# Two matrix products on one tensor engine: their matmuls put one by one in turn, with one order of passes for both

## The chip, the cores and the metric

The kernel runs on one core of a Trainium2 chip. A core has a tensor engine (PE; its loads of the stationary operand are shown apart as PEld), a vector engine (DVE, VectorE), a scalar engine (ACT, ScalarE), GpSimd (POOL), the sync engine's DMA queue (SP), and two on-chip memories: SBUF for operands and PSUM, eight banks into which the tensor engine accumulates. The metric is the device time of one execution in microseconds, as the median of several runs.

## The reference

For each of 4 batches with 6080 tokens of 256 channels, q and k are normalised over the tokens, a 256 x 256 attention over channels is formed and applied to v, and the 24320 resulting rows go through a feed-forward layer with 2048 hidden units and an ELU:

```python
qn = q / (np.linalg.norm(q, axis=1, keepdims=True) + 1e-06)
kn = k / (np.linalg.norm(k, axis=1, keepdims=True) + 1e-06)
a = softmax(kn.transpose(0, 2, 1) @ qn / tau)      # 256 x 256 a batch
x = (v @ a).reshape(24320, 256)
h = x @ w_in                                       # 256 -> 2048
g = np.where(h > 0.0, h, np.exp(np.minimum(h, 0.0)) - 1.0)
out = g @ w_out                                    # 2048 -> 256
```

## The kernel before

(v @ a) @ w_in is computed as v @ (a @ w_in), so each batch needs its own W' = a @ w_in (tiles `wp`). The tokens are cut into 12 chunks a batch, 8 of 512 tokens and 4 of 496, and a chunk is worked on in 16 *steps*, one for each 128 of the 2048 hidden units. There are 48 x 16 = 768 steps. The first three chunks take their first 8 steps one chunk after the other and then the last 8, while the weights are still being converted from 64-bit floats (`convert_w_in`, `convert_w_out`, on DVE and ACT).

The large products are made of three passes. Every operand is split into a high and a low part (`split`, L70 to L72: ACT casts the high part, DVE subtracts to get the low one), and high x high, high x low and low x high are added up in PSUM. A step i consists of:

- the first product, `h_item`: for each of two halves of the 256 channels three matmuls (L297 to L299) into a PSUM tile `ph`, whose stationary operand is a part of W' and whose moving operand is a part of v's chunk (`vt`);
- `elu`: on odd steps, and in all steps of the first three chunks, ACT computes a Relu and an Exp (L308, L309) and DVE joins them with ph (L310); on the others ACT computes one Exp (L312) and DVE does two operations (L313, L314). The last of these is the last reader of ph;
- `split_g` of the step before: ACT casts `e` to g's high part (L71), DVE subtracts to get g's low part (L72);
- the second product, `out_item`, of step j = i - 3 (LAG = 3): for each of two halves of the 256 outputs three matmuls (L334 to L336) into the PSUM tiles `po`, with w_out's parts (`wo`) as the stationary operand and g's as the moving one;
- after a chunk's last step, `store`: two copies out of po (L351; L347 and L349 in a few chunks) and the output DMAs.

Beside these, *side work* for the next batch is hung on some steps: row groups of q and k (24 a batch: a square and a split on ACT, a sum and a split on DVE: L120, L124, L71, L72; then `gram` matmuls, L142 and L145), the softmax over channels (L164 to L216), and the W' products (`pw`, L256 to L260). The loads of all these are issued by SP.

PSUM's eight banks are shared out as two for gram, three for the ring `w` (ph, pw and the softmax's small tiles) and three for the ring of po, two of which a chunk uses.

The program order is that of the loop at the end of the kernel. The framework then orders each engine's instructions by its own estimate of when they can start, so the order on ACT and DVE isn't exactly that of the code. Each engine runs its instructions strictly in order and waits at each for the semaphores of the engines that it depends on.

Of the kernel before, what the change touches and what calls it, by code (L numbers as in the profile page):

```python
# [7 lines left out]
F32 = mybir.dt.float32  # L8
# [6 lines left out]
# The high words of float64's 2**-126 and of the largest below 2**128, as float32 bits.  # L15
# [13 lines left out]
def channel_attention_then_elu_ffn(ctx: ExitStack, tc, q, k, vT, tau, w_in, w_out, outT):  # L29
    """out = elu((v @ softmax(kn^T qn / tau)) @ w_in) @ w_out.  # L30

    (v @ a) @ w_in is computed as v @ (a @ w_in): a is only C x C per batch.
    float32 operands of the large products are split exactly into two float32r
    parts, x = hi + lo (12 significant bits each), and three passes carry
    hi*hi + hi*lo + lo*hi. w_in and w_out come as the bits of float64 numbers
    and are rounded to float32 here. vT and outT have channels first: C x (B * N).
    """
# [14 lines left out]
    # The first M chunks take the first half of F, one after the other, and then the second:  # L52
    # w_out and half of w_in are converted while they run.
# [21 lines left out]
    def to_f32(dst, pair, act=False):  # L75
        """dst [P, n] float32 from pair [P, n, 2] words, low word first."""
# [4 lines left out]
        # the magnitude, held within float32's normal range (the words compare as floats do)  # L81
# [6 lines left out]
        # sign and top exponent bit stay; three exponent bits go  # L88
# [60 lines left out]
    def keep_warm(n):  # L149
        """Products that nothing reads: the tensor engine's clock falls while it waits."""  # L150
# [117 lines left out]
    def span(c):  # L268
        """The chunk's batch, first token and length."""
# [20 lines left out]
    def h_item(c, f, vt):  # L290
        b, _, n = span(c)
        wp = wps[b]
        ph = ps.tile([P, CH], F32, tag="w", bufs=WB, name="ph")
        fs = slice(f * P, f * P + P)
        for kt in range(KT):
            hi, lo = (vt[:, kt, x, 0:n] for x in range(2))
            nc.tensor.matmul(ph[:, 0:n], wp[kt][:, 0, fs], hi, start=(kt == 0), stop=False)  # L297
            nc.tensor.matmul(ph[:, 0:n], wp[kt][:, 0, fs], lo, start=False, stop=False)  # L298
            nc.tensor.matmul(ph[:, 0:n], wp[kt][:, 1, fs], hi, start=False, stop=(kt == KT - 1))  # L299
        return ph  # L300

    def elu(c, ph, both):
# [3 lines left out]
        # h > 0: h >= exp(0) - 1; h <= 0: exp(h) - 1 >= h  # L306
# [22 lines left out]
    def out_item(c, f, g, po):  # L329
        n = span(c)[2]  # L330
        hi, lo = (g[:, x, 0:n] for x in range(2))
        for dt in range(DT):
            o, ds = po[dt][:, 0:n], slice(dt * P, dt * P + P)
            nc.tensor.matmul(o, wo[:, f, 0, ds], hi, start=first(c, f), stop=False)  # L334
            nc.tensor.matmul(o, wo[:, f, 1, ds], hi, start=False, stop=False)  # L335
            nc.tensor.matmul(o, wo[:, f, 0, ds], lo, start=False, stop=last(c, f))  # L336
# [53 lines left out]
    # the second W' buffer's room until batch 1 needs it  # L390
# [150 lines left out]
    for i in range(len(steps) + LAG):  # L541
        if i < len(steps):
            c, f = steps[i]
            ph = h_item(c, f, vts[c])
# [3 lines left out]
        j = i - LAG  # L548
        if j >= 0:
            c, f = steps[j]  # L550
            if first(c, f):
                pos[c] = [
                    ps.tile([P, CH], F32, tag="o", bufs=8 - KT - WB, name=f"po_{c}_{dt}") for dt in range(DT)
                ]
            out_item(c, f, gs.pop(j), pos[c])
            if last(c, f):
                store(c, f, pos.pop(c))
# [37 lines left out]
```

## Time and profile before

| | before |
|---|---|
| median of 3 runs | 2319.38 us (2317.86 to 2319.63) |
| span of the profiled execution | 2318.7 us |
| PE busy | 2307.7 us, 10296 matmuls |
| PEld busy | 1909.2 us, 10296 loads |
| DVE busy | 1539.6 us |
| ACT busy | 1479.0 us |
| DMA | 118.14 MB |

The profiled execution's own time is its span, 2318.7 us, from the first to the last instruction; the median of the runs is 0.7 us above it. In the timeline a row gives the start and the duration in us, the engine, the source line, the operation, out<-in, and, in square brackets, how long the engine had been idle before and what ended that. The matmuls' durations overlap, since they are pipelined: how fast they follow one another is read from their starts. In a group's row the number behind the bar's comma is the mean duration in ns, and the last column the idle time of the engine just before.

### The profile page before, as it was taken

Reading aid. Unit: us, or ns where it says so; the run is one execution under the profiler, and the core shown is the slowest. Engines: PE = TensorE matmul, PEld = TensorE weight load, DVE = VectorE, ACT = ScalarE, POOL = GpSimd, SP = SyncE. Lnnn points to the kernel's source line nnn. Section 1 sums busy time; section 2 is a strip of 40 time slices with the busy share of each in tenths; the row PEclk is TensorE's granted clock in tenths of the full one; section 3 lists DMA queues with packets and bytes.
Section 4 is the critical chain, followed back from the end, with each engine's and each line's share of the span. In section 5 each row is a group of like instructions: output and inputs, shape, how many; then the busy total and the mean of one; then the engine's idle time right before and its main releaser. Section 6 shows DMA issues by size and latency. Waiting matters only on the chain.

```text
span 2318.7 us, 27257 instructions
## 1 busy us (share of the span) xinstructions
PE 2307.7 (100%) x10296; PEld 1909.2 (82%) x10296; DVE 1539.6 (66%) x2400; ACT 1479.0 (64%) x2413; POOL 3.1 (0%) x10
## 2 busy tenths in 40 slices
PE   8999999999999999999999999999999999999999
PEld 7778888888888888888888888888888888888887
DVE  7976666666766666666666666666666566665565
ACT  5776666666656666666666666666666666666665
POOL 0000000000000000000000000000000000000000
PEclk9999999999999999999999999999999999999999
DMA  9311121111201111111111111121101000000000
GB/s 335 107 37 46 55 64 55 64 52 37 64 19 55 55 46 55 55 47 51 37 55 37 46 46 55 46 63 46 48 31 56 26 19 27 28 19 10 19 9 18
DMA packets 60947, 118.14 MB, mean 51 GB/s; under 512 B 6032, under 2 KB 15760, under 8 KB 60816
## 3 DMA queue, kind: packets, MB, share of 16 engines
q1 hardware_dynamic: 60816, 116.42, 15.4%
q8 instruction: 80, 1.31, 0.2%
q14 instruction: 51, 0.42, 0.1%
HBM read 89.39 MB, written 27.00 MB: 50 GB/s over the span
## 4 chain that ended last, share of the span: by engine, by line
PE 97%; DVE 1%; DMA 1%; issue 0%; SPq 0%; ACT 0%; DVEq 0%
PE po L335 15%; PE po L334 15%; PE ph L297 15%; PE po L336 15%; PE ph L299 15%; PE ph L298 15%; PE gram L142 3%; PE gram L145 1%; DVE acc L124 1%; PE pw L256 1%; PE pw L258 0%; PE pw L260 0%; PE pw L259 0%; DMA wi<-in_moe_w_in_dram 0%; DMA raw<-in_k_dram 0%; PE pn L164 0%
## 5 line engine op out<-in xcount | busy, mean ns | idle before, releaser
L71 ACT CAST g<-e 128x512 fp32r<-128x512 f32 (+1 forms) x768 | 472.1, 615 | 509.9 <-DVE e L314 282.7
L72 DVE TENSOR_TENSOR g<-e,g 128x512 fp32r<-128x512 f32 (+1 forms) x768 | 526.2, 685 | 345.7 <-ACT g L71 308.3
L335 PE MATMUL po<-g,wo 128*128 128x512 f32 (+1 forms) x1536 | 603.1, 393 | 0.0
L334 PE MATMUL po<-g,wo 128*128 128x512 f32 (+1 forms) x1536 | 599.9, 391 | 0.0
L336 PE MATMUL po<-g,wo 128*128 128x512 f32 (+1 forms) x1536 | 597.9, 389 | 0.0
L297 PE MATMUL ph<-vt,wp 128*128 128x512 f32 (+1 forms) x1504 | 589.1, 392 | 0.0
L299 PE MATMUL ph<-vt,wp 128*128 128x512 f32 (+1 forms) x1504 | 584.4, 389 | 0.0
L298 PE MATMUL ph<-vt,wp 128*128 128x512 f32 (+1 forms) x1504 | 583.8, 388 | 0.0
L310 DVE SCALAR_TENSOR_TENSOR e<-e,ph 128x512 f32<-128x512 f32 (+1 forms) x408 | 278.0, 681 | 315.6 <-ACT e L309 315.1
L308 ACT ACTIVATE e<-ph 128x512 f32<-128x512 f32 (+1 forms) x408 | 242.6, 595 | 170.9 <-PE ph L299 168.1
L336 PEld LDWEIGHTS po<-g,wo 128*128 128x128 f32 x1536 | 289.3, 188 | 61.6
L334 PEld LDWEIGHTS po<-g,wo 128*128 128x128 f32 x1536 | 288.4, 188 | 61.2 <-ACT wo L71 0.4
L335 PEld LDWEIGHTS po<-g,wo 128*128 128x128 f32 x1536 | 288.7, 188 | 58.6 <-DVE wo L72 0.2
L297 PEld LDWEIGHTS ph<-vt,wp 128*128 128x128 f32 x1504 | 282.3, 188 | 61.5 <-issue 0.5
L299 PEld LDWEIGHTS ph<-vt,wp 128*128 128x128 f32 x1504 | 282.6, 188 | 59.0
L298 PEld LDWEIGHTS ph<-vt,wp 128*128 128x128 f32 x1504 | 283.0, 188 | 53.9 <-issue 1.0
L312 ACT ACTIVATE e<-ph 128x512 f32<-128x512 f32 (+1 forms) x360 | 213.3, 592 | 90.9 <-PE ph L299 72.8
L309 ACT ACTIVATE e<-e 128x512 f32<-128x512 f32 (+1 forms) x408 | 256.5, 629 | 12.1
L314 DVE TENSOR_TENSOR e<-ph,e 128x512 f32<-128x512 f32 (+1 forms) x360 | 246.6, 685 | 10.9
L313 DVE TENSOR_SCALAR e<-e 128x512 f32<-128x512 f32 (+1 forms) x360 | 152.1, 423 | 57.7 <-ACT e L312 55.2
L142 PE MATMUL gram<-qk 128*128 128x512 f32 x288 | 106.4, 393 | 0.0
L124 DVE TENSOR_TENSOR acc<-acc,sq 128x1024 f32<-128x1024 f32 x80 | 97.7, 1221 | 11.6 <-ACT sq L120 11.5
(94 smaller groups left out, 1130.2 us busy)
## 6 DMA issues: line engine op xcount, KB each, us to landing
raw<-in_q_dram SPq DMA_DIRECT2D x92, 256.0 KB, 2.7
raw<-in_k_dram SPq DMA_DIRECT2D x92, 256.0 KB, 3.0
v<-in_v_dram SPq DMA_DIRECT2D x32, 512.0 KB, 3.7
out_dram<-o SPq DMA_DIRECT2D x58, 256.0 KB, 2.0
v<-in_v_dram SPq DMA_DIRECT2D x16, 496.0 KB, 3.6
out_dram<-o SPq DMA_DIRECT2D x32, 248.0 KB, 2.1
wraw<-w_scr SPq DMA_DIRECT2D x12, 512.0 KB, 3.3
wi<-in_moe_w_in_dram SPq DMA_DIRECT2D x4, 1024.0 KB, 8.7
```

Of the source, the lines that this page charges most:

```text
L71: nc.scalar.copy(hi, src)
L72: nc.vector.tensor_sub(lo, src, hi.bitcast(F32))
L297: nc.tensor.matmul(ph[:, 0:n], wp[kt][:, 0, fs], hi, start=(kt == 0), stop=False)
L298: nc.tensor.matmul(ph[:, 0:n], wp[kt][:, 0, fs], lo, start=False, stop=False)
L299: nc.tensor.matmul(ph[:, 0:n], wp[kt][:, 1, fs], hi, start=False, stop=(kt == KT - 1))
L308: nc.scalar.activation(ev, pv, AF.Relu, scale=-1.0)
L309: x = nc.scalar.activation(ev, ev, AF.Exp, scale=-1.0)
L310: y = nc.vector.scalar_tensor_tensor(ev, ev, -1.0, pv, op0=ALU.add, op1=ALU.max)
L314: y = nc.vector.tensor_tensor(ev, pv, ev, op=ALU.max)
L334: nc.tensor.matmul(o, wo[:, f, 0, ds], hi, start=first(c, f), stop=False)
L335: nc.tensor.matmul(o, wo[:, f, 1, ds], hi, start=False, stop=False)
L336: nc.tensor.matmul(o, wo[:, f, 0, ds], lo, start=False, stop=last(c, f))
```

## The change

`h_item` and `out_item` no longer issue their matmuls. They return them as lists of six calls, and a new function `weave` issues the two lists in turn: the first product's first matmul, the second product's first, the first's second, and so on. Where only one list is there (the first three steps, and the last three rounds of the loop), it is issued alone. The second product's three passes used to be high x high, low weight x high, high weight x low; they now stand in the first product's order, high x high, high weight x low, low weight x high. In the loop the matmuls of both products now stand ahead of `elu` and `split_g`, and `store` behind them. The numbers of matmuls, operands, tiles and buffers stay the same.

```diff
     def h_item(c, f, vt):
...
+        calls = []
         for kt in range(KT):
             hi, lo = (vt[:, kt, x, 0:n] for x in range(2))
-            nc.tensor.matmul(ph[:, 0:n], wp[kt][:, 0, fs], hi, start=(kt == 0), stop=False)
-            nc.tensor.matmul(ph[:, 0:n], wp[kt][:, 0, fs], lo, start=False, stop=False)
-            nc.tensor.matmul(ph[:, 0:n], wp[kt][:, 1, fs], hi, start=False, stop=(kt == KT - 1))
-        return ph
+            for x, (w, m) in enumerate(((0, hi), (0, lo), (1, hi))):
+                calls.append(
+                    lambda kt=kt, x=x, w=w, m=m: nc.tensor.matmul(
+                        ph[:, 0:n],
+                        wp[kt][:, w, fs],
+                        m,
+                        start=(kt == 0 and x == 0),
+                        stop=(kt == KT - 1 and x == 2),
+                    )
+                )
+        return ph, calls
...
     def out_item(c, f, g, po):
...
         for dt in range(DT):
-            o, ds = po[dt][:, 0:n], slice(dt * P, dt * P + P)
-            nc.tensor.matmul(o, wo[:, f, 0, ds], hi, start=first(c, f), stop=False)
-            nc.tensor.matmul(o, wo[:, f, 1, ds], hi, start=False, stop=False)
-            nc.tensor.matmul(o, wo[:, f, 0, ds], lo, start=False, stop=last(c, f))
+            ds = slice(dt * P, dt * P + P)
+            for x, (w, m) in enumerate(((0, hi), (0, lo), (1, hi))):
+                calls.append(
...
+                )
+        return calls
+
+    def weave(a, b):
+
+        for x in range(max(len(a), len(b))):
+            for calls in (a, b):
+                if x < len(calls):
+                    calls[x]()
...
     for i in range(len(steps) + LAG):
+        firsts, seconds = [], []
         if i < len(steps):
             c, f = steps[i]
-            ph = h_item(c, f, vts[c])
+            ph, firsts = h_item(c, f, vts[c])
+        j = i - LAG
+        if j >= 0:
+            cj, fj = steps[j]
...
+            seconds = out_item(cj, fj, gs.pop(j), pos[cj])
+        weave(firsts, seconds)
+        if i < len(steps):
             es[i], *done = elu(c, ph, c < M or f % 2 == 1)
         if 0 <= i - 1 < len(steps):
             gs[i - 1] = split_g(steps[i - 1][0], es.pop(i - 1))
-        j = i - LAG
-        if j >= 0:
...
-            out_item(c, f, gs.pop(j), pos[c])
-            if last(c, f):
-                store(c, f, pos.pop(c))
+        if j >= 0 and last(cj, fj):
+            store(cj, fj, pos.pop(cj))
```

How this moves instructions is shown at three places. First TensorE in an ordinary step of chunk 13 (`ph` is the first product's tile, `po_13_0` and `po_13_1` the second's, `g` its moving operand; the semaphores that an instruction waits for stand in brackets, by the engine that raises them). Before:

```order
L297 MATMUL ph_5796<-vt_13_5376,wp_1_0_4629 128x512 [waits DVE_49]
L298 MATMUL ph_5796<-vt_13_5376,wp_1_0_4629 128x512
L299 MATMUL ph_5796<-vt_13_5376,wp_1_0_4629 128x512
L297 MATMUL ph_5796<-vt_13_5376,wp_1_1_4630 128x512
L298 MATMUL ph_5796<-vt_13_5376,wp_1_1_4630 128x512
L299 MATMUL ph_5796<-vt_13_5376,wp_1_1_4630 128x512
L334 MATMUL po_13_0_5600<-g_5759,wo_73 128x512 [waits Activation_49]
L335 MATMUL po_13_0_5600<-g_5759,wo_73 128x512
L336 MATMUL po_13_0_5600<-g_5759,wo_73 128x512 [waits DVE_49]
L334 MATMUL po_13_1_5601<-g_5759,wo_73 128x512
```

And now:

```order
L301 MATMUL ph_5820<-vt_13_5376,wp_1_0_4629 128x512 [waits DVE_49]
L347 MATMUL po_13_0_5587<-g_5789,wo_73 128x512 [waits Activation_49]
L301 MATMUL ph_5820<-vt_13_5376,wp_1_0_4629 128x512
L347 MATMUL po_13_0_5587<-g_5789,wo_73 128x512 [waits DVE_49]
L301 MATMUL ph_5820<-vt_13_5376,wp_1_0_4629 128x512
```

The wait for g's high part (raised by ScalarE) has moved from the 7th matmul of a step to the 2nd, the wait for its low part (VectorE) from the 9th to the 4th, and the last matmul into ph from the 6th to the 11th.

Second, ScalarE at the softmax of batch 1 (`e<-ph` is the elu's exponential, `a<-gram` the copies L206, `y<-pn` the square root L175, with a table load before it and another behind it). Before:

```order
L312 ACTIVATE e_4574<-ph_4567 128x496 [waits PE_49]
L206 COPY a_1_4613<-gram_1_0_1677 128x256
L206 COPY a_1_4613<-gram_1_1_1678 128x256
L175 ACT_TABLE_LOAD
L175 ACTIVATE y_4596<-pn_4587 128x4 [waits PE_49]
L179 ACT_TABLE_LOAD
```

And now:

```order
L321 ACTIVATE e_4580<-ph_4567 128x496 [waits PE_49]
L175 ACT_TABLE_LOAD
L175 ACTIVATE y_4596<-pn_4587 128x4 [waits PE_49]
L179 ACT_TABLE_LOAD
L179 ACTIVATE nm_4598<-ones_71 128x2
L206 COPY a_1_4613<-gram_1_0_1677 128x256
```

The two copies out of gram have moved behind both table loads; on VectorE the two additions L207 that need them moved from ahead of L182 to behind L198.

Third, ScalarE at the end of chunk 40 (`o<-po` are the copies of `store`, `g<-e` the high part of g). Before:

```order
L309 ACTIVATE e_15998<-e_15998 128x512 [waits Activation_49]
L71 CAST g_16022<-e_15998 128x512 [waits DVE_49]
L312 ACTIVATE e_16018<-ph_16011 128x512 [waits PE_49]
L351 COPY o_16031<-po_40_0_15716 128x512 [waits DMAHW6_49,DMAHW5_49,PE_49]
L351 COPY o_16031<-po_40_1_15717 128x512 [waits PE_49]
```

And now:

```order
L318 ACTIVATE e_16004<-e_16004 128x512 [waits Activation_49]
L377 COPY o_16031<-po_40_0_15703 128x512 [waits DMAHW6_49,DMAHW5_49,PE_49]
L71 CAST g_16028<-e_16004 128x512 [waits DVE_49]
L321 ACTIVATE e_16024<-ph_16011 128x512 [waits PE_49]
L377 COPY o_16031<-po_40_1_15704 128x512 [waits PE_49]
```

The first copy has moved ahead of the step's exponential and of the cast before it; the second stays behind the exponential.

More of the change, by code (lines that the diff above doesn't have):

```diff
@@ L331, in out_item @@
         hi, lo = (g[:, x, 0:n] for x in range(2))
+        calls = []
         for dt in range(DT):
-            o, ds = po[dt][:, 0:n], slice(dt * P, dt * P + P)
-            nc.tensor.matmul(o, wo[:, f, 0, ds], hi, start=first(c, f), stop=False)
-            nc.tensor.matmul(o, wo[:, f, 1, ds], hi, start=False, stop=False)
-            nc.tensor.matmul(o, wo[:, f, 0, ds], lo, start=False, stop=last(c, f))
+            ds = slice(dt * P, dt * P + P)
+            for x, (w, m) in enumerate(((0, hi), (0, lo), (1, hi))):
+                calls.append(
+                    lambda dt=dt, ds=ds, x=x, w=w, m=m: nc.tensor.matmul(
+                        po[dt][:, 0:n],
+                        wo[:, f, w, ds],
+                        m,
+                        start=(first(c, f) and x == 0),
+                        stop=(last(c, f) and x == 2),
+                    )
+                )
+        return calls
[4 more added lines that the diff above has]
+                    calls[x]()
     def store(c, f, po):
@@ L541, in channel_attention_then_elu_ffn @@
     for i in range(len(steps) + LAG):
+        firsts, seconds = [], []
         if i < len(steps):
             c, f = steps[i]
-            ph = h_item(c, f, vts[c])
+            ph, firsts = h_item(c, f, vts[c])
+        j = i - LAG
+        if j >= 0:
+            cj, fj = steps[j]
+            if first(cj, fj):
+                pos[cj] = [
+                    ps.tile([P, CH], F32, tag="o", bufs=8 - KT - WB, name=f"po_{cj}_{dt}") for dt in range(DT)
+                ]
+            seconds = out_item(cj, fj, gs.pop(j), pos[cj])
+        weave(firsts, seconds)
+        if i < len(steps):
             es[i], *done = elu(c, ph, c < M or f % 2 == 1)
```

5 lines of the change are left out of this document (removed).

## The prediction, made before the run

> **What bounds the kernel now.** I read the page from the top, then the chain of waits, then TensorE's groups by form and the timeline of single engines.
>
> ```profile
> span 2318.7 us, 27257 instructions
> ...
> PE 2307.7 (100%) x10296; PEld 1909.2 (82%) x10296; DVE 1539.6 (66%) x2400; ACT 1479.0 (64%) x2413; POOL 3.1 (0%) x10
> ...
> PE 97%; DVE 1%; DMA 1%; issue 0%; SPq 0%; ACT 0%; DVEq 0%
> ```
>
> ```profile
> L335 PE MATMUL po<-g,wo 128*128 128x512 f32 x1024 | 403.2, 394 | 0.0
> ...
> L335 PE MATMUL po<-g,wo 128*128 128x496 f32 x512 | 199.9, 390 | 0.0
> ```
>
> TensorE is busy for the whole span, 97% of the chain that ended last is its own, and its product groups show no idle time before them (the last column). So the time is TensorE's number of matmuls times its pace, and the change can act in two ways only: by another pace, or by waits that are not there now. The number of matmuls stays. L335 runs twice in a step: 1024 / 2 = 512 steps work on 512 tokens and 512 / 2 = 256 on 496, each with 12 product matmuls, so 6144 and 3072 of the two lengths.
>
> The durations in those rows overlap; the pace is read from starts. The timeline of TensorE, first for a stretch of 512-token steps without side work, whose first and last start stand 111 steps apart, then for one of 496-token steps, 56 steps long:
>
> ```profile
> 1831.36 0.39 PE L297 MATMUL ph<-vt,wp 128*128 128x512 f32 x1
> ...
> 2101.96 0.39 PE L297 MATMUL ph<-vt,wp 128*128 128x512 f32 x1
> ...
> 2103.10 0.39 PE L299 MATMUL ph<-vt,wp 128*128 128x512 f32 x1
> 2103.32 0.39 PE L334 MATMUL po<-g,wo 128*128 128x512 f32 x1
> ...
> 2134.76 0.39 PE L297 MATMUL ph<-vt,wp 128*128 128x512 f32 x1
> ```
>
> ```profile
> 2153.78 0.39 PE L297 MATMUL ph<-vt,wp 128*128 128x496 f32 x1
> ...
> 2305.35 0.39 PE L297 MATMUL ph<-vt,wp 128*128 128x496 f32 x1
> ...
> 2306.69 0.39 PE L334 MATMUL po<-g,wo 128*128 128x496 f32 x1
> ```
>
> (2134.76 - 1831.36) / 111 = 2.733 us a step, 227.8 ns a matmul; (2305.35 - 2153.78) / 56 = 2.707 us, 225.6 ns. Over the starts between these rows the first product's six take 226.5 ns each and the second's 229.0 at 512 tokens, 223.5 and 227.6 at 496. I call 0.2275 us a slot below.
>
> **The change, part by part.**
>
> *The pace.* Nothing in the trace of before alternates matmul by matmul, but two starts in each step do cross from one product to the other: L299 to L334 (2103.10 to 2103.32 above) and L336 to L297. Over the same two stretches these crossings take 225.8 and 226.7 ns at 512 tokens, 225.0 and 226.7 at 496, means 226.2 and 225.8. Inside the second product, with the accumulator unchanged, a start follows after 230.4 and 227.7 ns. After the change nearly all starts are crossings, so I take their means: 6144 x (226.2 - 227.8) = -9.8 us and 3072 x (225.8 - 225.6) = +0.6 us, together -9 us. The bounds come from the two products' own paces: all at the first product's is 6144 x (-1.3) + 3072 x (-2.1) = -14 us, all at the second's 6144 x 1.2 + 3072 x 2.0 = +14 us.
>
> The new pass order parts two passes that now follow each other with one stationary part (L297, L298). That costs nothing, because nothing is reused today:
>
> ```profile
> L298 PEld LDWEIGHTS ph<-vt,wp 128*128 128x128 f32 x1504 | 283.0, 188 | 53.9 <-issue 1.0
> ```
>
> There is one load for each L298 matmul (32 more stand in a group of their own), and its 188 ns lie under the 227 of the matmul before it. The Trainium skill (TensorE: Matmul & The Clock Gate, Part 2, step 1) says that separating the load from the matmul lets a kernel load once and multiply repeatedly. By that rule the change would give up one reuse for each of the 1536 L298 matmuls, 1536 x 188 ns = 0.29 ms of loading; in this trace the loads are as many as the matmuls (x10296 of each), so by the rows the term is zero.
>
> *The cover of the activation chain.* A step's first product is now complete at its 11th matmul, not its 6th: VectorE and ScalarE get it 5 slots, 1.14 us, later. The second product three steps on reads g's high part at its 2nd matmul, not its 7th, and the low part at its 4th, not its 9th: again 1.14 us. So the cover shrinks by 2.28 us everywhere. From the start of the last first-product matmul to that of the first reader of g's low part it was 39 slots (8.9 us) and is now 29 (6.6 us). What must fit in, for the step whose last first-product matmul starts at 2103.10 (timelines of ScalarE and VectorE):
>
> ```profile
> 2103.52 0.60 ACT L308 ACTIVATE e<-ph 128x512 f32<-128x512 f32 x1 [0.25 <-PE ph L299]
> 2104.15 0.63 ACT L309 ACTIVATE e<-e 128x512 f32<-128x512 f32 x1
> 2105.54 0.62 ACT L71 CAST g<-e 128x512 fp32r<-128x512 f32 x1 [0.75 <-DVE e L310]
> ```
>
> ```profile
> 2104.82 0.69 DVE L310 SCALAR_TENSOR_TENSOR e<-e,ph 128x512 f32<-128x512 f32 x1 [0.83 <-ACT e L309]
> 2106.19 0.69 DVE L72 TENSOR_TENSOR g<-e,g 128x512 fp32r<-128x512 f32 x1 [0.69 <-ACT g L71]
> ```
>
> 2106.88 - 2103.10 = 3.8 us of 6.6, so an ordinary step keeps 2.8 us and pays nothing. Going so through all 768 steps with the starts of before (end of L72 on g, plus 1.14 us, against the fourth matmul of step i+3), seven come late, by 4.6 us in all: three times 1.2 us and three times 0.2 us around the softmax of batches 1 to 3, once 0.4 us at step 7. The tightest steps with a row group keep about 1 us. The accumulator buffers have room too: the elu above releases ph at 2105.51, 4.65 us before step i+3 starts (2101.96 + 3 x 2.733 = 2110.16), and 3.5 us stay; where a W' product takes a buffer of the same ring in each step, ph must be free 19 slots, 4.3 us, after its last matmul starts, and it is after 2105.51 - 2103.10 = 2.4.
>
> *The softmax steps.* The low part of the step before the softmax waits behind the whole softmax on VectorE:
>
> ```profile
> 572.81 0.59 ACT L312 ACTIVATE e<-ph 128x496 f32<-128x496 f32 x1
> ...
> 573.95 1.28 ACT L175 ACT_TABLE_LOAD   x1
> 575.85 0.17 ACT L175 ACTIVATE y<-pn 128x4 f32<-128x4 f32 x1 [0.62 <-PE pn L164]
> ```
>
> ```profile
> 581.65 0.67 DVE L72 TENSOR_TENSOR g<-e,g 128x496 fp32r<-128x496 f32 x1
> ```
>
> ```profile
> 581.57 0.39 PE L297 MATMUL ph<-vt,wp 128*128 128x496 f32 x1
> ```
>
> In the new order the two copies L206 stand behind the table loads. The exponential before the load ends 1.14 us later, at 573.40 + 1.14 = 574.5, the load at 575.8, and the root at 575.85 loses nothing; the two additions L207, moved behind L198, fill VectorE's wait for TensorE before L210. So the subtraction still ends near 582.33, and its reader, now the fourth matmul of the step that starts at 581.57, is due at 581.57 + 3 x 0.225 = 582.25: 0.1 us late, not 1.2. I take 0.5 us for the three batches (from 0 to the 4.2 of the shift).
>
> *Start, chunk ends, tail.* In the first steps w_out is converted just in time:
>
> ```profile
> 91.20 0.62 ACT L71 CAST wo<-of 128x512 fp32r<-128x512 f32 x1 [0.19 <-DVE of L96]
> ```
>
> ```profile
> 91.87 0.74 PE L334 MATMUL po<-g,wo 128*128 128x512 f32 x2
> ```
>
> The high part lands 0.05 us before its reader, which now comes 1.14 us sooner; ten first-product matmuls run ahead there in the new order. I take 1 us (0 to 1.5) for the start. At a chunk's end 41 of 47 first copies now stand ahead of that step's elu, so the accumulators come free sooner; the six others could each be up to 0.8 us late; 0.5 us (0 to 5). At the tail the same chain, for a 496-token step whose last first-product matmul is
>
> ```profile
> 2303.76 0.39 PE L299 MATMUL ph<-vt,wp 128*128 128x496 f32 x1
> ```
>
> ```profile
> 2306.80 0.68 DVE L72 TENSOR_TENSOR g<-e,g 128x496 fp32r<-128x496 f32 x1 [0.67 <-ACT g L71]
> ```
>
> takes 2307.48 - 2303.76 = 3.7 us. Behind the eleventh matmul of the last step come one more of that step, two second products of six, and the high part's: the reader of the low part is the 15th, 3.4 us later, so 0.3 us late. Waits together: 0.5 + 1 + 0.5 + 0.3 = 2.3 us, from 0 to 11.
>
> *Sum.* 2318.7 - 9 + 2.3 = 2312 us of span; the median of the runs is 0.7 us above this execution's span, so 2313 us.
>
> **The rivals.**
>
> *The pass order sets the pace.* The first product's order of passes goes with its better pace at both lengths; if the order is the cause, the second product takes it over: -14 us, 2318.7 - 14 + 2.3 + 0.7 = 2308 us. For it: the gap between the products at 496 tokens (4.1 ns). Against: within the second product it is the unchanged accumulator that goes with slow starts at 512 tokens, which points to crossings.
>
> *Alternation paces all matmuls like the slower product.* Each load of one product's stationary part now lies under the other's stream, so the slower of the two may set both: +14 us, 2318.7 + 14 + 2.3 + 0.7 = 2336 us, slower. It decides once the mean start-to-start is above 227.8 and 225.6 ns. For it: the pace at 496 tokens barely follows the length, so it is not the stream alone that sets it. Against: the crossings above.
>
> *The cover is too short in the row groups.* Those steps keep about 1 us. A group's work on VectorE comes in two pieces of this length, the sum and the split:
>
> ```profile
> L124 DVE TENSOR_TENSOR acc<-acc,sq 128x1024 f32<-128x1024 f32 x80 | 97.7, 1221 | 11.6 <-ACT sq L120 11.5
> ```
>
> If one piece more comes ahead of g there, each of the 72 groups waits 0.2 us: 16 us on top, 2329 us, slower. It decides once that margin is under zero. Against: in the new order g's subtraction has more than 1.5 us of other work between it and its elu in 87 steps, in the old in 86.
>
> *The clock.*
>
> ```profile
> core 0: 2318.7 us, clock 0.999
> ```
>
> The clock stands at full with three changes of accumulator in each step. The product matmuls are 9216 x 0.227 = 2092 us, so each per cent of clock is 21 us: 2334 us for one. The Trainium skill (TensorE: Matmul & The Clock Gate, A second HAM failure mode: psum-queue depth-cycling) tells of a kernel that cycled through PSUM banks, idled briefly between groups and lost its clock; here the cycling becomes four times as frequent, but the idle time that the rule needs is not in the rows of this case.
>
> *Nothing changes but the waits*: 2318.7 + 2.3 + 0.7 = 2322 us.
>
> **How the numbers follow.** A measurement of this kernel tells about 0.2% from no change: below 2314.7 counts as faster, above 2324.0 as slower. My forecast (2313, its own range 2306 to 2320) has 0.42, of it 0.25 faster, 0.15 the same, 0.02 slower. The pass order has 0.17 (0.15 faster, 0.02 the same), the slower pace 0.18 and the short cover 0.15 (slower), the clock 0.02 (slower), only the waits 0.06 (0.05 the same, 0.01 slower). Sums: faster 0.40, same 0.22, slower 0.38. The range for 8 in 10 must hold both signs: 2303 to 2338, from a little under the pass-order case to a little over the slower pace.
>
> **What would show it.** In the profile after, twelve starts in the last batch should take 2.715 us at 512 tokens and 2.71 at 496; 2.72 and 2.68 would speak for the pass order, 2.75 and 2.73 for the slower pace. TensorE's groups should still show next to no idle time before them except a few tenths at the softmax and in the first 100 us; idle time before the second product's matmuls, ended by VectorE's g L72, spread over the row groups, would mean that the cover was too short. A granted clock below 0.99 would show the last case. The forecast is wrong if the mean pace inside the weave does not lie near that of the crossings.

## The result, and the profile after

| | before | after |
|---|---|---|
| median of 21 runs each | 2320.14 us (2317.84 to 2325.37) | 2323.86 us (2321.74 to 2327.85) |
| ratio to before | | 1.0017, 95% interval 1.0011 to 1.0024 |
| span of the profiled execution | 2318.7 us | 2325.5 us |

The change costs 3.7 us, 0.17%: small, but the interval of the ratio lies wholly above 1, and it is the other way than the forecast of 2313 us. The page of the profile after, its totals, the chain of waits by engine and by line, and the two product groups (count, busy time and mean ns, then idle time before them):

```profile
span 2325.5 us, 27249 instructions
PE 2313.3 (99%) x10296; PEld 1909.2 (82%) x10296; DVE 1537.3 (66%) x2400; ACT 1473.0 (63%) x2413; POOL 3.1 (0%) x10
...
PE 98%; DMA 1%; DVE 1%; SPq 0%; issue 0%; ACT 0%; DVEq 0%
...
L347 PE MATMUL po<-g,wo 128*128 128x512 f32 (+1 forms) x4608 | 1792.7, 391 | 0.0
L301 PE MATMUL ph<-vt,wp 128*128 128x512 f32 (+1 forms) x4512 | 1752.2, 390 | 0.0
```

The kind of bound has not changed: the same 10296 matmuls and loads, TensorE 98% of the chain, no idle time ahead of either product. So the difference must lie in the pace, and that is read from starts. The timeline of TensorE after, for the same steps as in the prediction: the first matmul of the 593rd and the 704th step (512 tokens, 111 steps apart), and of the 711th and the 767th (496 tokens, 56 apart):

```profile
1837.81 0.39 PE L301 MATMUL ph<-vt,wp 128*128 128x512 f32 x1
...
2144.17 0.40 PE L301 MATMUL ph<-vt,wp 128*128 128x512 f32 x1
...
2163.05 0.39 PE L301 MATMUL ph<-vt,wp 128*128 128x496 f32 x1
...
2312.01 0.39 PE L301 MATMUL ph<-vt,wp 128*128 128x496 f32 x1
```

(2144.17 - 1837.81) / 111 = 2.760 us a step at 512 tokens, where before it was 2.733; (2312.01 - 2163.05) / 56 = 2.660 us at 496, where it was 2.707. One change, two lengths, two signs: if all steps ran so, 512 x 0.027 = 13.8 us would be lost and 256 x 0.047 = 12.0 us won.

The profiled execution of after also began its first product 3.1 us later, in the loads ahead of it, which the change does not touch; in the profiles of the first two experiments below this start lies at 65.4 and 69.4 us, so it varies by itself. So the two executions are compared from the first product's first matmul to TensorE's end, here before and then after:

```profile
66.22 0.58 PE L297 MATMUL ph<-vt,wp 128*128 128x512 f32 x1
...
2314.62 0.39 PE L336 MATMUL po<-g,wo 128*128 128x496 f32 x1
```

```profile
69.33 0.58 PE L301 MATMUL ph<-vt,wp 128*128 128x512 f32 x1
...
2319.15 2.67 PE L347 MATMUL po<-g,wo 128*128 128x496 f32 x10
```

2315.01 - 66.22 = 2248.79 us and 2321.82 - 69.33 = 2252.49 us: 3.7 us, as in the medians. The two paces alone would give 13.8 - 12.0 = 1.8 us of it, but not all steps run at them. Summed from start to start as the steps ran, the first 48 take 0.8 us more than before, the 455 later steps with both products at 512 tokens 9.6 us more, the 243 with both at 496 tokens 6.7 us less, and the steps that mix the two lengths (-0.2) and the end (+0.2) cancel. The gain at 496 tokens is short of its pace because many steps miss it: of the 167 with twelve matmuls and nothing beside them, 133 take 2.660 us and the others 2.68 to 2.81. At 512 tokens, on the other side, 53 of 347 such steps ran at 2.760 before already.

### The profile page after: what moved, and what is told of

Its sections match the earlier page's. It is cut to its first block, busy times and chain, and to the rows that moved or that the text cites. A ratio compares the mean times of both kernels' runs of the same rounds, so it can differ in the third digit from the quotient of the medians.

```text
span 2325.5 us, 27249 instructions
## 1 busy us (share of the span) xinstructions
PE 2313.3 (99%) x10296; PEld 1909.2 (82%) x10296; DVE 1537.3 (66%) x2400; ACT 1473.0 (63%) x2413; POOL 3.1 (0%) x10
## 4 chain that ended last, share of the span: by engine, by line
PE 98%; DMA 1%; DVE 1%; SPq 0%; issue 0%; ACT 0%; DVEq 0%
PE po L347 45%; PE ph L301 45%; PE gram L142 3%; PE gram L145 1%; DMA raw<-in_k_dram 1%; PE gram L451 1%; PE pw L256 1%; PE pw L260 0%; PE pw L259 0%; PE pw L258 0%; DMA wi<-in_moe_w_in_dram 0%; PE pn L164 0%; DVE acc L124 0%; SPq L109 0%; PE pt L223 0%
## 5 line engine op out<-in xcount | busy, mean ns | idle before, releaser
L120 ACT ACTIVATE sq<-raw 128x1024 f32<-128x1024 f32 x84 | 88.3, 1051 | 5.0 <-DVE acc L124 3.0
L72 DVE TENSOR_TENSOR qk<-raw,qk 128x1024 fp32r<-128x1024 f32 x72 | 87.8, 1219 | 0.5 <-ACT qk L71 0.5
L145 PE MATMUL gram<-qk 128*128 128x256 f32 x288 | 80.9, 281 | 0.0
L71 ACT CAST qk<-raw 128x1024 fp32r<-128x1024 f32 x72 | 74.7, 1037 | 0.0
L142 PEld LDWEIGHTS gram<-qk 128*128 128x128 f32 x288 | 54.2, 188 | 11.6
L72 DVE TENSOR_TENSOR vt<-v,vt 128x512 fp32r<-128x512 f32 (+1 forms) x94 | 63.6, 678 | 0.0
L145 PEld LDWEIGHTS gram<-qk 128*128 128x128 f32 x288 | 54.4, 189 | 5.7
L377 ACT COPY o<-po 128x512 f32<-128x512 f32 (+1 forms) x89 | 50.9, 580 | 9.4 <-PE po L347 9.4
```

The lines of the kernel that those rows point to most:

```text
L71: nc.scalar.copy(hi, src)
L72: nc.vector.tensor_sub(lo, src, hi.bitcast(F32))
L142: nc.tensor.matmul(pg, hl[:, 0, 1, r, cs], hl[:, :, 0, r, :], start=(first and r == 0), stop=False)
L145: nc.tensor.matmul(pg[:, 0, :], hl[:, 1, 1, r, cs], hl[:, 0, 0, r, :], start=False, stop=(last and r == 1))
```

## The experiments

All twelve runs follow; "step" is the time between the first matmuls of neighbouring steps, and where nothing else is said it is the mean over the 111 and 56 steps named above.

**The two parts apart.** The weave with the second product's old pass order:

```diff
-            for x, (w, m) in enumerate(((0, hi), (0, lo), (1, hi))):
+            for x, (w, m) in enumerate(((0, hi), (1, hi), (0, lo))):
```

> The weave with the second product's old order of passes. If the taking in turn alone sets the new pace, an ordinary step in the last batch takes 2.76 us at 512 tokens and 2.66 at 496 as in the changed kernel, and the time is that of the changed kernel, about 2324 us. If the order of passes makes it, the steps go back to 2.733 and 2.707 us and the time to about 2320 us.

The kernel before with the new pass order alone:

```diff
             nc.tensor.matmul(o, wo[:, f, 0, ds], hi, start=first(c, f), stop=False)
-            nc.tensor.matmul(o, wo[:, f, 1, ds], hi, start=False, stop=False)
-            nc.tensor.matmul(o, wo[:, f, 0, ds], lo, start=False, stop=last(c, f))
+            nc.tensor.matmul(o, wo[:, f, 0, ds], lo, start=False, stop=False)
+            nc.tensor.matmul(o, wo[:, f, 1, ds], hi, start=False, stop=last(c, f))
```

> The kernel before with only the second product's order of passes changed. If the order of passes sets a product's pace, the second product takes over the first's 226.5 and 223.5 ns: steps of 2.72 and 2.68 us, 512 x 0.014 + 256 x 0.024 = 13 us less, about 2307 us. If only the taking in turn counts, steps stay at 2.733 and 2.707 us and the time at 2320 us.

And the kernel before with its second product's matmuls alternating between its two accumulators, still one product behind the other:

```diff
-        for dt in range(DT):
-            o, ds = po[dt][:, 0:n], slice(dt * P, dt * P + P)
...
+        for x, (w, m) in enumerate(((0, hi), (1, hi), (0, lo))):
+            for dt in range(DT):
+                o, ds = po[dt][:, 0:n], slice(dt * P, dt * P + P)
+                nc.tensor.matmul(o, wo[:, f, w, ds], m, start=(first(c, f) and x == 0), stop=(last(c, f) and x == 2))
```

> The kernel before, with the second product's six matmuls taking its two accumulators in turn (each pass for both halves of the outputs before the next pass); the products themselves stay apart. If a change of accumulator after every matmul is what changes the pace, the second product's six take about 230 ns each at 512 tokens and 222 at 496 as in the weave: steps of 6 x 226.5 + 6 x 230 = 2.74 and 6 x 223.5 + 6 x 221.7 = 2.67 us, about 2320 + 512 x 0.007 - 256 x 0.037 = 2314 us. If the accumulators do not matter, the steps stay at 2.733 and 2.707 us and the time at 2320 us.

| kernel | median | ratio, 95% interval | step at 512 | step at 496 |
|---|---|---|---|---|
| before | 2320.1 us | | 2.733 us | 2.707 us |
| after | 2323.9 us | 1.0017 (1.0011 to 1.0024) | 2.760 us | 2.660 us |
| weave alone | 2323.3 us | 1.0015 (1.0006 to 1.0023) | 2.760 us | 2.660 us |
| pass order alone | 2320.0 us | 1.0001 (0.9992 to 1.001) | 2.733 us | 2.707 us |
| accumulators alternate | 2321.2 us | 1.0003 (0.9994 to 1.0012) | 2.733 us | 2.707 us |

The timeline of TensorE for the kernel with alternating accumulators shows how exact this is:

```profile
1831.22 0.39 PE L297 MATMUL ph<-vt,wp 128*128 128x512 f32 x1
...
2134.62 0.39 PE L297 MATMUL ph<-vt,wp 128*128 128x512 f32 x1
```

That is 303.40 us for 111 steps, and 303.40 between the same starts before (2134.76 - 1831.36). So neither the order of the passes nor how often the accumulator changes has any part in the pace of product order, and with the weave the steps are 2.760 and 2.660 us in either order of passes. The weave has all of it.

**The weave only where it gains.** Chunks of 496 tokens woven, those of 512 in product order:

```diff
-        weave(firsts, seconds)
+        short = i < len(steps) and span(c)[2] < CH
+        weave(firsts, seconds if short else [])
...
+            if not short:
+                weave([], seconds)
```

> The changed kernel, but woven only in steps whose first product works on 496 tokens; the other steps issue the first product's matmuls, then the second's, with the new order of passes. If the pace belongs to the order of matmuls and the length, and is reached within a few matmuls, 496-token steps take 2.66 us and 512-token steps 2.733 (2.72 if the order of passes helps): 256 x 0.047 = 12 us less than before, and about 5 us given back in the steps with side work as in the changed kernel, so 2309 to 2315 us. If the gain at 496 depends on what ran long before, no step is at 2.66 and the time is 2320 us or more.

2313.7 us, ratio 0.9969 (0.9958 to 0.9981), with steps of 2.733 us at 512 tokens and 2.660 at 496. The two effects are independent, and the half that gains beats both kernels.

**Is it the length, the load, or a rhythm?** 13 chunks of many lengths, and both orders in each:

```diff
-    sizes = chunk_sizes(N, CH)
+    sizes = [512, 508, 504, 500, 496, 488, 480, 472, 464, 448, 432, 416, 360]
...
-        weave(firsts, seconds)
+        short = i < len(steps) and f >= 9
+        weave(firsts, seconds if short else [])
...
+        if not short:
+            weave([], seconds)
```

> Each batch's 6080 tokens are cut into 13 chunks of 512, 508, 504, 500, 496, 488, 480, 472, 464, 448, 432, 416 and 360 tokens; in each chunk the first nine steps keep the products one behind the other, the last seven weave them. Only the pace per length and order in the last batch is read; the total time (13 chunks, so 8% more matmuls) says nothing. Known: in product order 227.8 ns a matmul at 512 tokens and 225.6 at 496, woven 230.0 and 221.7. Theory A, the load sets the floor: the next stationary load starts 3 ns after a matmul's start, takes 188 ns, and the next matmul starts 31 to 40 ns after the load's end, at both lengths; so in product order the pace hardly follows the length and stays within 220 to 228 ns down to 360 tokens, and woven it falls to about 220 and stays there too. Theory B, the length sets it, with a fixed addition that the order decides: the pace falls by about the same ns for each token everywhere, at least 0.4 ns for one, so that 448 tokens take 205 ns or less and 360 tokens 170 or less in both orders. Theory C, a matter of phases between engine parts: no smooth line, jumps of 3 ns and more up and down between neighbouring lengths, and the sign of woven minus product order changes more than once between 512 and 480.

The step in the last batch, once it repeats (in us; where two values alternate, as woven at 512 and 464 tokens and in product order at 416, their mean):

| tokens | 512 | 508 | 504 | 500 | 496 | 488 | 480 | 472 | 464 | 448 | 432 | 416 | 360 |
|---|---|---|---|---|---|---|---|---|---|---|---|---|---|
| product order | 2.733 | 2.753 | 2.747 | 2.660 | 2.707 | 2.687 | 2.613 | 2.560 | 2.520 | 2.447 | 2.347 | 2.256 | 1.973 |
| woven | 2.760 | 2.760 | 2.747 | 2.680 | 2.720 | 2.740 | 2.600 | 2.560 | 2.510 | 2.427 | 2.400 | 2.280 | 1.960 |

Some of its rows, four steps apart: 508 tokens in product order, 500 in product order, 496 woven, and 360 woven:

```profile
1858.13 0.39 PE L301 MATMUL ph<-vt,wp 128*128 128x508 f32 x1
...
1869.15 0.39 PE L301 MATMUL ph<-vt,wp 128*128 128x508 f32 x1
...
1945.93 0.39 PE L301 MATMUL ph<-vt,wp 128*128 128x500 f32 x1
...
1956.57 0.39 PE L301 MATMUL ph<-vt,wp 128*128 128x500 f32 x1
...
2005.05 0.39 PE L301 MATMUL ph<-vt,wp 128*128 128x496 f32 x1
...
2015.92 0.39 PE L301 MATMUL ph<-vt,wp 128*128 128x496 f32 x1
...
2321.56 0.33 PE L301 MATMUL ph<-vt,wp 128*128 128x360 f32 x1
...
2329.40 0.33 PE L301 MATMUL ph<-vt,wp 128*128 128x360 f32 x1
```

(1956.57 - 1945.93) / 4 = 2.660 us at 500 tokens, while four tokens fewer take 2.707 and eight more 2.75. The first mark of theory C is there, no smooth line, with jumps of up to 0.087 us a step (7 ns a matmul) between neighbours. Its second is not, as far as the table goes: woven is the slower or equal order from 512 down to 488 tokens, and the sign turns only at 480 (and again at 432 and at 360). Theory A falls with the last pair, (2329.40 - 2321.56) / 12 / 4 = 163 ns a matmul, less than a load's 188 ns. The loads then overlap one another (the timeline of the weight loads at 360 tokens):

```profile
2322.05 0.19 PEld L301 LDWEIGHTS ph<-vt,wp 128*128 128x128 f32 x1
2322.22 0.19 PEld L347 LDWEIGHTS po<-g,wo 128*128 128x128 f32 x1
```

so 188 ns is how long a load takes, not how often one can start. Theory B gives the broad line (163 ns at 360 tokens, 228 to 230 at 512) but not the steps on it. One reading was not expected by any theory: woven 496-token steps took 2.720 us here, against 2.660 in the changed kernel, with the same instructions. With that 2.660 the sign would turn three times between 512 and 480 tokens, so the second mark of theory C isn't settled by one row of the table.

**How often must the products change?** Twos, threes, and one by one with the second product first, in one kernel:

```diff
-    def weave(a, b):
+    def weave(a, b, size=1):
+        if size < 0:
+            a, b, size = b, a, 1
...
-        weave(firsts, seconds)
+        size = 6 if i >= len(steps) else 2 if f < 5 else 3 if f < 10 else -1
+        weave(firsts, seconds if size != 6 else [], size)
```

> Chunks as in the changed kernel; in each chunk the first five steps alternate two matmuls of one product with two of the other, the next five three with three, the last six one with one, but the second product's first. Only the paces in the last batch are read. If each change of product costs (theory: crossings), the pace lies between the known ends by the share of crossings, which are 2 of 12 in product order, 4 of 12 in threes, 6 of 12 in twos, 12 of 12 woven: at 512 tokens 227.8 + 2.2 x (2/10) = 228.2 in threes and 228.7 in twos, at 496 225.6 - 3.9 x (2/10) = 224.8 in threes and 224.0 in twos. If the rhythm counts and not the crossings (rival), threes or twos lie outside the span between the ends (227.8 to 230.0, 225.6 to 221.7) or at one of them. Woven with the second product first: the crossings are the same, so 230.0 and 221.7 within 0.3 by both.

TensorE's timeline: threes at 512 and at 496 tokens, each pair three steps apart, then one by one with the second product first at 496, two steps apart:

```profile
1853.86 0.39 PE L301 MATMUL ph<-vt,wp 128*128 128x512 f32 x1
...
1862.21 0.40 PE L301 MATMUL ph<-vt,wp 128*128 128x512 f32 x1
...
2207.38 0.39 PE L301 MATMUL ph<-vt,wp 128*128 128x496 f32 x1
...
2215.46 0.38 PE L301 MATMUL ph<-vt,wp 128*128 128x496 f32 x1
...
2223.82 0.39 PE L301 MATMUL ph<-vt,wp 128*128 128x496 f32 x1
...
2229.30 0.39 PE L301 MATMUL ph<-vt,wp 128*128 128x496 f32 x1
```

Threes take 8.35 / 3 = 2.783 us at 512 tokens (2.787 once settled), 232 ns a matmul, slower than both ends; twos take 2.768 to 2.783, not yet steady within their five steps. At 496 threes take 2.693 us and twos 2.720, slower than product order. A price for each crossing would have put all of them between the ends, so it falls. Woven with the second product first, 496-token steps take 2.740 us in this chunk (5.48 / 2) and 2.720 in others, not the 2.660 that both theories expected, though in a row of such steps the matmuls alternate as in the changed kernel (only their partners are one place apart); at 512 they take 2.760.

**TensorE's own, or shared memory?** The changed kernel, and the kernel before, without the elu in the last batch, where the second product reads one fixed tile, `kept`, in place of g:

```diff
+            if c < NCH - NB:
-            es[i], *done = elu(c, ph, c < M or f % 2 == 1)
+                es[i], *done = elu(c, ph, c < M or f % 2 == 1)
...
-            gs[i - 1] = split_g(steps[i - 1][0], es.pop(i - 1))
+            gs[i - 1] = split_g(steps[i - 1][0], es.pop(i - 1)) if steps[i - 1][0] < NCH - NB else kept
```

> The changed kernel, but in the last batch (the last 192 steps) the elu and the split of its result are left out and the second product reads one fixed tile instead of g; ScalarE and VectorE do next to nothing there. Only the step in the last batch is read: 2.760 us at 512 tokens and 2.660 at 496 in the changed kernel. If the pace is TensorE's own rhythm, it stays at 2.760 and 2.660 (within 0.01, or at another of the values seen for the same length, 2.720 or 2.740 at 496). If it comes from sharing on-chip memory with ScalarE and VectorE, it falls at both lengths, and to at most 2.72 at 512 (the 226.5 ns of the first product in product order, the lowest seen at 512, twelve times).

> The same left out of the kernel before. TensorE's own rhythm: the step of the last batch stays at 2.733 us at 512 tokens and 2.707 at 496, and the second product keeps its 229.0 ns against the first's 226.5. Shared memory: the step falls below 2.72 and the second product, which reads what ScalarE and VectorE have just written, comes down to the first's pace.

The windows view of the two stretches, in the changed kernel and then without the elu (us, then busy time and count of PE, PEld, DVE, ACT and POOL, the granted clock, the DMAs' share and GB/s):

```profile
1838.00:2144.00 306.00, 306.00 (x1332) 249.94 (x1331) 184.46 (x291) 184.29 (x306) 0.00 (x0) 1.00 0.06 21
2163.00:2312.00 149.00, 149.00 (x673) 126.17 (x673) 90.38 (x147) 89.92 (x153) 0.00 (x0) 1.00 0.03 11
```

```profile
1836.00:2141.00 305.00, 305.00 (x1328) 249.14 (x1327) 8.81 (x14) 15.33 (x27) 0.00 (x0) 1.00 0.06 21
2161.00:2309.00 148.00, 148.00 (x670) 125.32 (x669) 2.52 (x4) 5.67 (x10) 0.00 (x0) 1.00 0.03 11
```

VectorE falls from 184 to 9 us and ScalarE from 184 to 15, and TensorE does not notice. In its timeline the stretches are (2141.53 - 1835.17) / 111 = 2.760 us and (2309.37 - 2160.41) / 56 = 2.660 us:

```profile
1835.17 0.39 PE L301 MATMUL ph<-vt,wp 128*128 128x512 f32 x1
...
2141.53 0.40 PE L301 MATMUL ph<-vt,wp 128*128 128x512 f32 x1
...
2160.41 0.39 PE L301 MATMUL ph<-vt,wp 128*128 128x496 f32 x1
...
2309.37 0.39 PE L301 MATMUL ph<-vt,wp 128*128 128x496 f32 x1
```

The kernel before without its elu keeps 2.733 and 2.707 us. The DMAs have no part either: in the changed kernel they are busy for a share of 0.00 from 2215 to 2225 us and of 0.14 from 2235 to 2245, and every step from 2163 to 2312 us takes 2.660. The pace is TensorE's own.

**Does the way in decide?** One small extra product, a *jolt*, that nothing reads, in each chunk of the last batch, in the changed kernel and in the kernel before. The trace shows each as two matmuls:

```diff
+    def jolt(n):
+        pd = ps.tile([P, P], F32, tag="w", bufs=WB, name="pd")
+        nc.tensor.matmul(pd[:, 0:n], ones, ones[:, 0:n], start=True, stop=True)
...
+            if f == 4 and c >= NCH - NB:
+                jolt(16 * (c - NCH + NB + 1) if c < NCH - 4 else 32 * (c - NCH + 5) - 16)
```

> The changed kernel with one more matmul, that nothing reads, ahead of the fifth step of each chunk of the last batch, of 16 to 128 columns by 16 in the eight chunks of 512 tokens and of 16, 48, 80 and 112 columns in the four of 496. Read: the step from the seventh of each chunk on. Theory, the way into a stretch decides its rhythm: with the same instructions after the jolt the step at 496 tokens is 2.660 us after some and 2.720 or 2.740 after others (the values seen where other steps went before), and at 512 it may leave 2.760. Rival, the sequence alone decides: 2.660 and 2.760 in every chunk; what was seen at 2.720 and 2.740 was then due to the other steps of those chunks.

> The same added to the kernel before. Entry decides: the step at 512 is 2.733 us after some jolts and 2.760 after others (53 of its 347 steps without side work run at 2.760 now), and at 496 it is 2.707, 2.720 or another. The sequence alone: 2.733 and 2.707 in every chunk.

TensorE's timeline in the third 496-token chunk of the last batch, from the 7th to the 15th step, first woven, then in product order:

```profile
2246.97 0.39 PE L305 MATMUL ph<-vt,wp 128*128 128x496 f32 x1
...
2268.72 0.39 PE L305 MATMUL ph<-vt,wp 128*128 128x496 f32 x1
```

```profile
2244.49 0.39 PE L301 MATMUL ph<-vt,wp 128*128 128x496 f32 x1
...
2266.14 0.39 PE L301 MATMUL ph<-vt,wp 128*128 128x496 f32 x1
```

Woven, 21.75 / 8 = 2.72 us a step where the changed kernel has 2.660, and this in all four chunks. No jolt among the 496-token steps did this: in the first of the four chunks the pace is there ahead of the chunk's own jolt, from the 5th to the 11th matmul of its fourth step:

```profile
2151.99 0.39 PE L305 MATMUL ph<-vt,wp 128*128 128x496 f32 x1
...
2153.35 0.39 PE L305 MATMUL ph<-vt,wp 128*128 128x496 f32 x1
```

(2153.35 - 2151.99) / 6 = 227 ns a matmul, which is 2.72 us in twelve; the changed kernel has 222 ns at the same place. What differs is what ran ahead, the 512-token steps with their eight jolts. The four jolts among the 496-token steps cost their own time and left the pace at 2.72. The changed kernel itself has both paces. In its 21st chunk, woven steps of 496 tokens take (1047.24 - 1039.08) / 3 = 2.720 us, and behind the gram matmuls of the next row group (1064.68 - 1056.70) / 3 = 2.660:

```profile
1039.08 0.39 PE L301 MATMUL ph<-vt,wp 128*128 128x496 f32 x1
...
1047.24 0.39 PE L301 MATMUL ph<-vt,wp 128*128 128x496 f32 x1
...
1056.70 0.39 PE L301 MATMUL ph<-vt,wp 128*128 128x496 f32 x1
...
1064.68 0.39 PE L301 MATMUL ph<-vt,wp 128*128 128x496 f32 x1
```

In product order 21.65 / 8 = 2.706 us, as without a jolt; the jolt costs its own time and one or two steps later all is as before. At 512 tokens both keep their 2.760 and 2.733. So for the woven order at 496 tokens the way in decides, and for product order, with these jolts, the sequence alone does: each expectation is half right.

**Better kernels.** By the table of lengths, 500 tokens in product order are a good length. The cut of each batch into seven chunks of 512 tokens, four of 500 and one of 496, with that one woven (the edit is shown against the kernel that weaves the chunks of 496):

```diff
-    sizes = chunk_sizes(N, CH)
+    sizes = [512] * 7 + [500] * 4 + [496]
...
-        short = i < len(steps) and span(c)[2] < CH
+        short = i < len(steps) and span(c)[2] < 500
```

> Chunks of 7 x 512, 4 x 500 and 496 tokens in place of 8 x 512 and 4 x 496, the 496 woven and all others in product order. From the steps of the run with many lengths (2.733 us at 512, 2.660 at 500 in product order; woven 2.660 at 496): per 16 steps 7 x 2.733 + 4 x 2.660 + 2.660 = 32.43 against 32.51 of the kernel that weaves four 496s, times 64 = 4.7 us less than its 2313.7, so 2309 us. If the 2.660 at 500 was one rhythm among several that the steps before it decide (rival), the 500s may run at 2.70 to 2.75 us, and the time is 2319 to 2332 (4 x 64 x 0.04 to 0.09 = 10 to 23 us more).

and the same cut in the kernel before, nothing woven:

```diff
-    sizes = chunk_sizes(N, CH)
+    sizes = [512] * 7 + [500] * 4 + [496]
```

> The kernel before with chunks of 7 x 512, 4 x 500 and 496 tokens in place of 8 x 512 and 4 x 496, in product order throughout, nothing woven. If the pace at 500 belongs to the product order itself, 7 x 2.733 + 4 x 2.660 + 2.707 = 32.48 us a 16 steps' set against 8 x 2.733 + 4 x 2.707 = 32.69 before: 64 x 0.21 = 13 us less by the pure rhythms, 2307; with the steps beside side work, which cost the woven and cut kernel 3 us over such a sum (it came to 2310.8 where its steps gave 2309 at most), 2307 to 2314. Rival, the cut helps only with the weave beside it: the 500s do not hold 2.660 and the time is 2317 or more.

The first took 2310.8 us, ratio 0.9956 (0.9943 to 0.997); the 500s hold their pace, and the rival falls. The second took 2312.1 us, ratio 0.9965 (0.9951 to 0.9978). Between the 695th and the 751st step, all of 500 tokens, the timeline of the second has

```profile
2104.50 0.39 PE L297 MATMUL ph<-vt,wp 128*128 128x500 f32 x1
...
2253.46 0.39 PE L297 MATMUL ph<-vt,wp 128*128 128x500 f32 x1
```

148.96 / 56 = 2.660 us. One line that cuts the tokens otherwise, without any weave, is worth as much as the weave at its best, as far as the intervals tell. Both stay behind the sums of their steps (2309 and 2307 us), because beside side work only 114 of 182 plain steps at 500 tokens run at 2.660 us and the others at up to 2.744.

## Why the prediction was wrong, point by point

- **What bounds the kernel**: right. TensorE's pace was everything, and the change could act through it alone.
- **The pace term, -9 us: the step that failed.** It took the starts that cross between the products in before (226.2 and 225.8 ns) as the pace of a kernel made of crossings. Measured, a woven matmul takes 2.760 / 12 = 230.0 ns at 512 tokens and 2.660 / 12 = 221.7 at 496: at these paces +13.8 and -12.0 us, and +9.6 and -6.7 as the steps behind the first 48 ran, instead of -9.8 and +0.6. The sign taken in favour of crossings, that the unchanged accumulator goes with slow starts, fell too: with alternating accumulators the steps were the same. The Trainium skill (TensorE: Matmul & The Clock Gate, Back-to-back issue gap) says that in a stream of loads and matmuls both set the spacing together, at a sustained figure of about 131 ns for 512 columns. The runs show 227.8 ns in product order and 230.0 woven, and none of them separates the loads' part. The start-to-start time of one place belongs to the rhythm of the whole sequence and cannot be carried to another: threes have 4 crossings among 12 starts, and are slower at 512 tokens than either end.
- **The bounds of the pace term**, from -14 to +14 us, held the sum, but not their parts: by length they ran from 6144 x (-1.3) = -8 to 6144 x 1.2 = +7 us at 512 tokens and from 3072 x (-2.1) = -6 to 3072 x 2.0 = +6 us at 496, and both lengths lay outside, with opposite signs, at the steady paces and as the steps ran. The total fell near no change because two large terms cancel, not because little happened.
- **The waits, 2.3 us**: 0.7 measured, by what starts more than 245 ns apart hold beyond a slot of 228 ns, against the same in before. The chunk ends, put at 0.5 us, are about right: six times the second product's first step in a chunk waits for ScalarE's copies out of the accumulators, 0.7 us in all. The start, put at 1 us, is mis-sized: there the first 48 steps grew by 0.8 us in all, and the slower pace alone would be 48 x 0.027 = 1.3. The softmax, put at 0.1 us late in each batch, is 0.16 us early: in batch 1 g's low part ends at 585.46 + 0.67 = 586.13 and its reader starts at 586.29, and in the next two batches the same 0.16 us are left (VectorE, then TensorE):

```profile
585.46 0.67 DVE L72 TENSOR_TENSOR g<-e,g 128x496 fp32r<-128x496 f32 x1
```

```profile
586.29 0.39 PE L347 MATMUL po<-g,wo 128*128 128x496 f32 x1
```

- **The tail**, put at 0.3 us late: right. The last low part is finished at 2319.92 + 0.68 = 2320.60 (VectorE), its reader is the matmul that the trace has from 2320.28 on, and the one behind it starts at 2320.65, 0.37 us after the reader where a slot is 0.22; with 0.11 at the next one that is 0.26 us:

```profile
2320.28 0.86 PE L347 MATMUL po<-g,wo 128*128 128x496 f32 x2
...
2320.65 0.72 PE L347 MATMUL po<-g,wo 128*128 128x496 f32 x2
```

```profile
2319.92 0.68 DVE L72 TENSOR_TENSOR g<-e,g 128x496 fp32r<-128x496 f32 x1 [0.68 <-ACT g L71]
```

- **The cover**: right. Predicted were 3.8 us from the start of a step's last first-product matmul to the end of g's low part, and 2.8 us left. In the timelines after it is 2122.65 - 2118.87 = 3.8 us, and 2125.53 - 2122.65 = 2.9 us are left:

```profile
2118.87 0.39 PE L301 MATMUL ph<-vt,wp 128*128 128x512 f32 x1
...
2125.53 0.40 PE L347 MATMUL po<-g,wo 128*128 128x512 f32 x1
```

```profile
2121.96 0.69 DVE L72 TENSOR_TENSOR g<-e,g 128x512 fp32r<-128x512 f32 x1 [0.69 <-ACT g L71]
```

- **No reuse of stationary parts lost**: right, x10296 loads as before.
- **The rivals.** The pass order sets nothing (shown by itself: ratio 1.0001). A pace like the slower product's, or slower, is what 512 tokens show (2.760 us, 2.75 said), and the opposite is what 496 show (2.660, where even the pass-order case said 2.68); no rival had a sign for each length. The short cover would have shown as a late start of g's readers; outside the softmax and the tail the least time left between g's low part and its reader is 0.8 us. *Nothing changes but the waits* came nearest, 2322 us against 2323.9, and by luck: the pace that it left alone moved at both lengths. The clock stands at 1.00 in the windows above with an accumulator changed at each matmul.
- **"Mean pace near the crossings"** was named as what the forecast hangs on, and it is what broke.

What makes the rhythm stays open. The runs exclude the order of passes, the changes of accumulator within the second product, the loads' own duration as a floor, VectorE and ScalarE, and the DMAs. They do not part what the weave alternates, for product, accumulator and moving operand change together at each of its matmuls; and what the tensor engine repeats inside, so that 500 tokens go faster than 496, no view of the profile shows.

## What to carry to other kernels

Where the tensor engine is the bound and its matmuls wait for nothing, measure the pace of the whole sequence, one step to the next, for each tile length apart: a mean over two lengths can hide two large effects of opposite sign, and the starts of single places do not carry to another order. Some lengths near the largest tile are several ns a matmul better or worse than their neighbours (here 221.7 ns at 500 tokens, 225.6 at 496), so a scan of the cut, one line, is worth as much here as the best reordering. A gain that hangs on the way into a stretch (496 tokens woven) can be lost by what runs ahead of it; one that the plain order shows after each disturbance can be counted on more.

## What was not expected of the hardware

- With full overlap of loads and no waits, the time of a step isn't monotonic in the length of its matmuls: in product order 2.733 us at 512 tokens, 2.753 at 508, 2.660 at 500, 2.707 at 496.
- The same sequence of woven matmuls at 496 tokens runs steadily at 2.660 or at 2.720 us a step, by what ran ahead of it. With the second product first it runs at 2.720 or 2.740.
- The steady steps are whole multiples of a 150th of a microsecond: 2.660, 2.707, 2.720, 2.733 and 2.760 us are 399, 406, 408, 410 and 414 of them.
- A weight load lasts 188 ns in the mean, yet loads start 163 ns apart when the matmuls have 360 columns.
